# Sending 120 of the last head's 128 output-weight rows to 24 partitions through three DMA engines

## Chip, cores, metric

One core of one Trainium2 chip. The metric is the device time of one execution in microseconds; the median of several executions is quoted, with the lowest and highest. The profile of an execution covers a span some 1.8 us shorter than its time.

## The reference

A decode step for four sequences: attention of 32 query heads over 8 key/value heads and a window of 1024 positions, an output projection `wo`, and beside it a small MLP whose result gates the attention's.

```python
xn = _layernorm(x)                       # x: (4, 1, 512)
s = _A_ref(xn, k_cache, v_cache, wq, wo) # q = xn @ wq; softmax(q k^T) v; ... @ wo, wo: (4096, 512)
g = _silu(_B_ref(xn, w1, b1, w2, b2))    # layernorm, w1, gelu, w2
return x + s * g
```

Some 28.8 MB are read: keys and values 16.8 MB, `wq` and `wo` 4.2 MB each, `w1` and `w2` 1.8 MB each. The tolerance of the comparison is wide against `s * g`. So "correct" says little about a row put in the wrong place.

## The kernel before

All large loads go through SyncE's DMA queue, one after the other: keys, values, MLP weights, and `wo` last. The 4096 rows of `wo` lie as eight groups (one per key/value head) of 128 partitions x 4 rows, in six loads; the last group is cut in two, so that less work follows the last landing.

```python
wo_r = A_wo.rearrange("(g p i) o -> p g i o", g=HKV, i=4)
for n, (g0, g1, i0, i1) in enumerate(((0, 2, 0, 4), (2, 4, 0, 4), (4, 6, 0, 4), (6, 7, 0, 4),
                                      (7, 8, 0, 3), (7, 8, 3, 4))):
    d_wo.append((g0, g1, i0, i1, pg.dma("sp", ...)))      # cut: the load of these groups and rows

def to_rows(g0, g1):         # attention output (128 dims x heads) -> the rows' order, on PE
    ...                      # cut: 16 matmuls with selector weights, then one copy to OW (DVE)

def wo(k, rows):             # a tile's four 128-column pieces are the weights, OW is streamed (4 columns)
    for g in range(g0, g1):
        for i in range(i0, i1):
            for c in range(4):
                pe.matmul(psM[:, PS_W + c * 4:PS_W + (c + 1) * 4],
                          wo_sb[:, g, i, c * 128:(c + 1) * 128], OW[:, i, g * 4:(g + 1) * 4], ...)
```

That is 16 selection matmuls and 128 output matmuls at the end of PE's work; then a product with the gate, a transpose, the sum with `x` and the store.

The softmax here doesn't subtract the row's maximum and nothing guards it: scores larger than these inputs give would overflow.

Of the kernel before, what the change touches and what calls it, by code (L numbers as in the profile page):

```python
# [16 lines left out]
class _Program:  # L17
# [10 lines left out]
    def add(self, eng, fn, *deps):  # L28
        op = _Op(eng, fn, deps)
        self.ops[eng].append(op)  # L30
        return op
# [42 lines left out]
def bass_recurrent_scan__sliding_block_cached__mixer_channel_mlp__decode_kernel(  # L74
# [14 lines left out]
    ALU = mybir.AluOpType  # L89
    AF = mybir.ActivationFunctionType  # L90
    AX = mybir.AxisListType
    BF16 = dt.bfloat16
    F32 = dt.float32

    B, D = 4, 512
    HQ, HKV, DH = 32, 8, 128
# [12 lines left out]
    NB = 3  # L109
# [6 lines left out]
    sb = nc.alloc_sbuf_tensor  # L116
# [5 lines left out]
    wo_sb = sb([128, HKV, 4, D], BF16)  # L122
    w1_sb = sb([128, 4, F], BF16)
    w2_sb = sb([128, FC, D], BF16)
    kt_buf = sb([128, NKT, UT * 128], BF16)
    P_buf = sb([128, HKV, NC * 16], BF16)

# [18 lines left out]
    ones_bf = sb([128, 128], BF16)  # L146
# [12 lines left out]
    b2_sb = sb([4, 128], BF16)  # L159
    sel = sb([128, 4, 32], BF16)  # L160
    OW = sb([128, 4, HKV * 4], BF16)
    hT = sb([128, 64], BF16)

    OTb = sb([128, HKV * 16], BF16)
# [10 lines left out]
    psS = [nc.alloc_psum_tensor("psS%d" % i, [128, 512], F32) for i in range(2)]  # L175
    psO = [nc.alloc_psum_tensor("psO%d" % i, [128, 512], F32) for i in range(2)]
    psM = nc.alloc_psum_tensor("psM", [128, 512], F32)
    PS_Z, PS_W = 192, 208

    pg = _Program(nc)  # L180
    add = pg.add
# [3 lines left out]
    d_b1 = pg.dma("act", "b1", lambda e: e.dma_start(  # L185
        b1_sb[0:1, :], B_b1.rearrange("(o n) -> o n", o=1)))
# [17 lines left out]
    def load_v(g):  # L204
        d_v[g] = pg.dma("sp", "v%d" % g, lambda e: e.dma_start(  # L205
            kv_buf[:, (HKV + g) % NS, :, :].rearrange("p c d -> p (c d)"), cache_rows(A_v_cache, g)),
            t_last[(HKV + g) % NS] if HKV + g >= NS else None)
# [11 lines left out]
    for g in range(2, HKV):  # L219
# [4 lines left out]
    c_1 = add("gp", lambda e: e.memset(ones_bf[:, :], 1.0))  # L224
    c_id = add("gp", lambda e: e.affine_select(
        ident[:, :], ones_bf[:, :], [[1, 128]], ALU.is_equal, 0.0,
        base=0, channel_multiplier=-1), c_1)
    c_ind = add("gp", lambda e: e.affine_select(
        ind[:, :], ones_bf[:, :], [[0, 32], [1, 4]], ALU.is_equal, 0.0,
        base=0, channel_multiplier=-1), c_1)  # L230
    c_sel = add("gp", lambda e: e.affine_select(
        sel[:, :, :], ones_bf[:, :], [[1, 4], [4, 32]], ALU.is_equal, 0.0,
        base=0, channel_multiplier=-1), c_1)
    c_xT = add("gp", lambda e: e.memset(xT[:, :, :], 0.0))
    c_yT = add("gp", lambda e: e.memset(yT[:, :, :], 0.0))
    c_z = add("gp", lambda e: e.memset(zero_bf[:, :], 0.0))
# [2 lines left out]
        base=0, channel_multiplier=-1), c_z)  # L239
    c_o32 = add("gp", lambda e: e.memset(ones32[:, :], 1.0))  # L240
    c_id32 = add("gp", lambda e: e.affine_select(
        ident32[:, :], ones32[:, :], [[1, 128]], ALU.is_equal, 0.0,
        base=0, channel_multiplier=-1), c_o32)


    v = add("dve", lambda e: e.tensor_copy(x32[:, :], x_bf[:, :]), d_x)  # L246
# [3 lines left out]
    a = add("act", lambda e: e.activation(sq1[:, :], vt1[:, :], AF.Sqrt), v)  # L250
# [9 lines left out]
    a = add("act", lambda e: e.activation(sq2[:, :], vt2[:, :], AF.Sqrt), v)  # L260
# [5 lines left out]
    cp = {}  # L266
    sc = {}
    ex = [None] * HKV
    den = [None] * HKV
    ep = [None] * HKV  # L270
# [54 lines left out]
    def epilogue(g):  # L325
        pso = psO[g % 2]
        cs = slice(g * 16, (g + 1) * 16)
        v = add("dve", lambda e: e.tensor_reduce(  # L328
            den_sb[:, cs], bass.AP(psS[g % 2], 0, [[512, 128], [1, 16], [16, NC]]),
            AX.X, ALU.add), den[g])  # L330
        v = add("dve", lambda e: e.reciprocal(rden[:, cs], den_sb[:, cs]), v)  # L331

        ep[g] = add("dve", lambda e: e.tensor_tensor(  # L333
            bass.AP(OTb, g * 16, [[HKV * 16, 128], [1, 4], [4, 4]]),
            pso[:, 0:16], rden[:, cs], ALU.mult), v, pv_op[g])


    v_xyT = None
# [3 lines left out]
    def f_xy(pe):  # L342
# [10 lines left out]
    v_xyT = add("dve", lambda e: e.tensor_copy(  # L353
        yT[:, :, 0:4], psK[1][:, 16:32].rearrange("p (c b) -> p c b", c=4)), t_xy, c_yT)
# [32 lines left out]
    mlp = {}  # L387

    def f32k(n):

        return kt_buf[:, n, :].bitcast(F32)
# [3 lines left out]
    def mlp1():  # L395
        def fn(pe):
            last = None
            for c in range(4):
                for s in range(4):
                    pe.matmul(psK[0][32 * s:32 * s + 32, 0:1024].bitcast(F32), yT[:, c, :],  # L400
                              bass.AP(w1_sb, c * F + K0[s], [[4 * F, 128], [1, 4], [FC, 128]]),
                              start=(c == 0), stop=False, tile_position=(0, 32 * s))
            for s in range(4):
                last = pe.matmul(psK[0][32 * s:32 * s + 32, 0:1024].bitcast(F32),
                                 ones_bf[0:1, 0:32],
                                 bass.AP(b1_sb, K0[s], [[F, 1], [1, 4], [FC, 128]]),
                                 start=False, stop=True, tile_position=(0, 32 * s))
            return last
        t = add("pe", fn, v_xyT, d_w1, d_b1, *[cp[n] for n in range(NUN - NB, NUN)])
        a = add("act", lambda e: e.activation(f32k(0), h_ps, AF.Square), t)  # L410
        v = add("dve", lambda e: e.scalar_tensor_tensor(f32k(1), f32k(0), 1.0 / GELU_K, h_ps,  # L411
                                                        op0=ALU.add, op1=ALU.mult), a)
        mlp["t"] = add("act", lambda e: e.activation(f32k(2), f32k(1), AF.Tanh,
                                                     scale=GELU_C * GELU_K), v)
# [41 lines left out]
    NUN = HKV * NU  # L456
    for n in range(LAG, NUN + LAG):
# [4 lines left out]
    d_w1 = pg.dma("sp", "w1", lambda e: e.dma_start(  # L462
        w1_sb[:, :, :], B_w1.rearrange("(p c) f -> p c f", c=4)))
# [2 lines left out]
        w2_sb[:, :, :], B_w2.rearrange("(p c) o -> p c o", c=FC)))  # L466
    for g in range(2, HKV):
        load_v(g)

    wo_r = A_wo.rearrange("(g p i) o -> p g i o", g=HKV, i=4)  # L470
    d_wo = []
    for n, (g0, g1, i0, i1) in enumerate(((0, 2, 0, 4), (2, 4, 0, 4), (4, 6, 0, 4), (6, 7, 0, 4),
                                          (7, 8, 0, 3), (7, 8, 3, 4))):
        d_wo.append((g0, g1, i0, i1, pg.dma("sp", "wo%d" % n, lambda e, g0=g0, g1=g1, i0=i0, i1=i1:
                                            e.dma_start(wo_sb[:, g0:g1, i0:i1, :],  # L475
                                                        wo_r[:, g0:g1, i0:i1, :]))))

    def to_rows(g0, g1):

        psx = psS[0]  # L480

        def fn(pe):
            last = None
            for i in range(4):
                for j in range(4):
                    last = pe.matmul(psx[32 * j:32 * j + 32, i * 32 + g0 * 4:i * 32 + g1 * 4],
                                     sel[:, i, :],
                                     bass.AP(OTb, g0 * 16 + j * 4,
                                             [[HKV * 16, 128], [16, g1 - g0], [1, 4]]),
                                     start=True, stop=True)  # L490
            return last
        t = add("pe", fn, ep[g1 - 1], c_sel, ex[HKV - 2])
        return add("dve", lambda e: e.tensor_copy(
            OW[:, :, g0 * 4:g1 * 4],
            psx[:, 0:128].rearrange("p (i n) -> p i n", i=4)[:, :, g0 * 4:g1 * 4]), t)

    first = [True]

    def wo(k, rows):
        g0, g1, i0, i1, d = d_wo[k]  # L500

        def fn(pe):
            last = None
            for g in range(g0, g1):
                for i in range(i0, i1):
                    for c in range(4):
                        last = pe.matmul(psM[:, PS_W + c * 4:PS_W + (c + 1) * 4],  # L507
                                         wo_sb[:, g, i, c * 128:(c + 1) * 128],
                                         OW[:, i, g * 4:(g + 1) * 4],
                                         start=first[0], stop=(k == len(d_wo) - 1 and i == i1 - 1),  # L510
                                         skip_group_check=True)
                        first[0] = False
            return last
        return add("pe", fn, d, rows, mlp["g"])

    for g in range(HKV):
        PV(g)
        if g == 0:
            epilogue(0)
            mlp1()  # L520
        if g >= 2:
            epilogue(g - 1)
        if g == 1:
            mlp2()
            mlp3()
        if g == 2:
            mlp4()
    epilogue(HKV - 1)
    rows = to_rows(0, HKV)
    for k in range(len(d_wo)):  # L530
        t_w = wo(k, rows)


    v = add("dve", lambda e: e.tensor_tensor(  # L534
# [3 lines left out]
    t = add("pe", lambda pe: pe.transpose(psS[0][0:16, 0:128], sg_sb[:, :], ident32[:, :]),  # L538
            v, c_id32, ex[HKV - 2])
# [56 lines left out]
```

## Time and profile before

| | before |
|---|---|
| time, median of 3 (lowest to highest) | 77.07 us (77.06 to 77.15) |
| span of the profile | 75.3 us |
| landing of the last `wo` load, first and last of 16 engines | 70.42 and 72.17 us |
| last output matmul starts | 72.32 us |
| PE busy, DMA queue busy | 66%, 92% |

Each of SyncE's large loads raises its semaphore 16 times, the page counts 16 DMA engines, and 16 packets of these loads are in flight (at 68.20 us). So I count one rise of the semaphore, a landing, as one engine; the landings in the table are the times of these rises in the trace. They tell how many engines are late, but not which. Lines of the page, the chain of waits, the tail's table and PE's timeline stand in the prediction, with their reading.

### The profile page before, as it was taken

Reading aid. Unit: us, or ns where it says so; the run is one execution under the profiler, and the core shown is the slowest. Engines: PE = TensorE matmul, PEld = TensorE weight load, DVE = VectorE, ACT = ScalarE, POOL = GpSimd, SP = SyncE. Lnnn points to the kernel's source line nnn. Section 1 sums busy time; section 2 is a strip of 40 time slices with the busy share of each in tenths; the row PEclk is TensorE's granted clock in tenths of the full one; section 3 lists DMA queues with packets and bytes.
Section 4 is the critical chain, followed back from the end, with each engine's and each line's share of the span. In section 5 each row is a group of like instructions: output and inputs, shape, how many; then the busy total and the mean of one; then the engine's idle time right before and its main releaser. Section 6 shows DMA issues by size and latency. Waiting matters only on the chain.

```text
span 75.3 us, 2297 instructions
## 1 busy us (share of the span) xinstructions
PE 50.0 (66%) x1046; PEld 39.8 (53%) x1058; DVE 39.3 (52%) x82; ACT 9.8 (13%) x16; POOL 4.6 (6%) x14
## 2 busy tenths in 40 slices
PE   0000039993859949987997994999069879818770
PEld 0000039992359939976997860104049576518740
DVE  0778107786058967985996424001664679770010
ACT  0611000000090303111130630003300000000000
POOL 6980000000000000000000000000000000000000
PEclk9999999999999999999999999569755555555555
DMA  1899999998999999999999999999999999999600
GB/s 36 244 455 405 420 422 479 435 444 370 427 422 431 422 418 431 427 414 466 401 420 453 406 443 390 427 431 409 427 427 440 418 401 416 418 420 416 252 25 2
DMA packets 4219, 28.99 MB, mean 385 GB/s; under 512 B 493, under 2 KB 625, under 8 KB 1650
## 3 DMA queue, kind: packets, MB, share of 16 engines
q1 hardware_dynamic: 4160, 28.84, 92.2%
q8 instruction: 8, 0.13, 0.6%
q10 hardware_dynamic: 50, 0.01, 0.1%
q14 instruction: 1, 0.01, 0.0%
HBM read 28.85 MB, written 0.00 MB: 383 GB/s over the span
## 4 chain that ended last, share of the span: by engine, by line
DMA 36%; PE 35%; SPq 16%; issue 5%; DVE 4%
DMA wo_sb<-in_A_wo_dram 24%; PE psK L278 22%; SPq L475 15%; DMA kv_buf<-in_A_k_cache_dram 12%; PE psS L297 7%; PE psO L362 3%; DVE kt_buf L284 2%; DVE q_sb L368 1%; PE psK L374 1%; PE psM L507 1%; PE psK L346 1%; PE psS L538 1%; SPq L212 1%; SPq L205 0%; DVE o_bf L540 0%
## 5 line engine op out<-in xcount | busy, mean ns | idle before, releaser
L278 PE MATMUL psK<-ident,kv_buf 128*128 128x128 bf16 x256 | 21.2, 237 | 11.8 <-DMA kv_buf<-in_A_k_cache_dram 10.6
L284 DVE COPY kt_buf<-psK 128x1024 bf16<-128x1024 bf16 x32 | 21.3, 691 | 8.7 <-PE psK L278 8.6
L278 PEld LDWEIGHTS psK<-ident,kv_buf 128*128 128x128 bf16 x256 | 17.1, 108 | 11.1 <-DMA kv_buf<-in_A_k_cache_dram 10.6
L297 PE MATMUL psS<-qT,kt_buf 128*128 128x16 bf16 x256 | 10.4, 169 | 1.7 <-issue 1.1
L297 PEld LDWEIGHTS psS<-qT,kt_buf 128*128 128x128 bf16 x256 | 9.4, 96 | 3.0 <-issue 2.1
L315 PEld LDWEIGHTS psO<-P_buf,kv_buf 128*128 128x128 bf16 x256 | 7.4, 102 | 3.0 <-issue 3.0
L315 PE MATMUL psO<-P_buf,kv_buf 128*128 128x16 bf16 x256 | 8.0, 173 | 1.0 <-DVE OTb L333 0.6
L328 DVE TENSOR_REDUCE den_sb<-psS 128x16 f32<-128x512 f32 x8 | 5.5, 691 | 4.2 <-PE psO L315 4.0
L305 ACT ACTIVATE P_buf<-psS 128x512 bf16<-128x512 f32 x8 | 4.8, 597 | 17.1 <-PE psS L297 17.1
L400 PE MATMUL psK<-w_sb,yT 128*32 128x512 bf16 x16 | 4.9, 1093 | 1.3 <-issue 1.3
L507 PE MATMUL psM<-OW,wo_sb 128*128 128x4 bf16 x128 | 3.9, 166 | 1.1 <-issue 0.6
L507 PEld LDWEIGHTS psM<-OW,wo_sb 128*128 128x128 bf16 x128 | 3.6, 104 | 1.4 <-issue 1.2
L411 DVE SCALAR_TENSOR_TENSOR kt_buf<-kt_buf,psK 128x512 f32<-128x512 f32 x1 | 0.7, 686 | 6.4 <-ACT kt_buf L410 6.4
L534 DVE TENSOR_TENSOR sg_sb<-psM,g_sb 128x16 f32<-128x16 f32 x1 | 0.2, 185 | 4.7 <-PE psM L507 4.7
L400 PEld LDWEIGHTS psK<-w_sb,yT 128*32 128x32 bf16 x16 | 0.5, 114 | 3.8 <-issue 3.8
L369 ACT ACTIVATE q_sb<-psO 128x512 bf16<-128x512 f32 x1 | 0.6, 597 | 13.5 <-PE psO L362 13.5
L424 PE MATMUL psK<-ident,kt_buf 128*128 128x128 bf16 x4 | 0.6, 307 | 2.4 <-DVE kt_buf L419 2.4
L331 DVE RECIPROCAL rden<-den_sb 128x16 f32<-128x16 f32 x8 | 2.0, 253 | 0.3
L362 PE MATMUL psO<-wq_sb,xT 128*32 128x512 bf16 x32 | 1.9, 380 | 0.3 <-DVE xT L351 0.3
L246 DVE CAST P_buf<-x_bf 4x512 f32<-4x512 bf16 x1 | 0.8, 795 | 2.4 <-DMA x_bf<-in_A_x_dram 2.4
L237 POOL TENSOR_SCALAR_AFFINE_SELECT negm<-zero_bf 128x512 bf16<-128x512 bf16 x1 | 1.9, 1852 | 0.1
L321 PE MATMUL psS<-P_buf,ones_bf 128*128 128x512 bf16 x3 | 1.8, 587 | 0.0
(64 smaller groups left out, 27.4 us busy)
## 6 DMA issues: line engine op xcount, KB each, us to landing
kv_buf<-in_A_k_cache_dram SPq DMA_DIRECT2D x8, 1024.0 KB, 19.9
kv_buf<-in_A_v_cache_dram SPq DMA_DIRECT2D x8, 1024.0 KB, 22.8
wq_sb<-in_A_wq_dram SPq DMA_DIRECT2D x2, 2048.0 KB, 11.3
w_sb<-in_B_w_dram SPq DMA_DIRECT2D x2, 1792.0 KB, 27.9
wo_sb<-in_A_wo_dram SPq DMA_DIRECT2D x3, 1024.0 KB, 24.3
wo_sb<-in_A_wo_dram SPq DMA_DIRECT2D x1, 512.0 KB, 21.5
wo_sb<-in_A_wo_dram SPq DMA_DIRECT2D x1, 384.0 KB, 18.2
wo_sb<-in_A_wo_dram SPq DMA_DIRECT2D x1, 128.0 KB, 18.0
```

Source lines behind the costliest of these rows:

```text
L237: c_neg = add("gp", lambda e: e.affine_select(negm[:, :], zero_bf[:, :], [[0, 32], [1, 4], [0, 4]], ALU.is_equal, NEG, base=0, channel_mul ...
L278: last = pe.transpose(psK[n % NB][:, j * 128:(j + 1) * 128], kv_buf[:, g, u * UT + j, :], ident[:, :])
L284: cp[n] = add("dve", lambda e: e.tensor_copy(kt_buf[:, n % NKT, :], psK[n % NB][:, 0:1024]), t, sc.get(n - NKT))
L297: last = pe.matmul(psS[g % 2][:, c * 16:(c + 1) * 16], kt_buf[:, n % NKT, j * 128:(j + 1) * 128], qT[:, g * 16:(g + 1) * 16], start=False, ...
L305: ex[g] = add("act", lambda e: e.activation(P_buf[:, g, :], psS[g % 2][:, 0:512], AF.Exp, scale=SCALE), sc[n])
L315: last = pe.matmul(pso[:, 0:16], kv_buf[:, (HKV + g) % NS, c, :], P_buf[:, g, c * 16:(c + 1) * 16], start=(c == 0), stop=(c == NC - 1))
L328: v = add("dve", lambda e: e.tensor_reduce(den_sb[:, cs], bass.AP(psS[g % 2], 0, [[512, 128], [1, 16], [16, NC]]), AX.X, ALU.add), den[g])
L331: v = add("dve", lambda e: e.reciprocal(rden[:, cs], den_sb[:, cs]), v)
L362: last = pe.matmul(psO[m // 4][32 * s:32 * s + 32, 0:512], xT[:, c, :], wq_sb[:, c, m * 512:(m + 1) * 512], start=(c == 0), stop=(c == 3), ...
L400: pe.matmul(psK[0][32 * s:32 * s + 32, 0:1024].bitcast(F32), yT[:, c, :], bass.AP(w1_sb, c * F + K0[s], [[4 * F, 128], [1, 4], [FC, 128]]) ...
L475: e.dma_start(wo_sb[:, g0:g1, i0:i1, :], wo_r[:, g0:g1, i0:i1, :]))))
L507: last = pe.matmul(psM[:, PS_W + c * 4:PS_W + (c + 1) * 4], wo_sb[:, g, i, c * 128:(c + 1) * 128], OW[:, i, g * 4:(g + 1) * 4], start=firs ...
```

## The change

Half of the DMA engines finish some 1.4 us ahead of the others: the last load's landings before are eight at 70.42 to 70.73 us and eight at 71.37 to 72.17. The change takes the 128 rows of the last head from the load that all 16 engines share, and gives 120 of them to a load on three engines, meant to be ones that finish early. The load has 24 partitions of five rows; its source pattern has an outer size of 3. The other eight rows go by a small load. The group's other three heads then lie as three rows per partition. The buffer is that of the first MLP weights, so these loads wait for the matmuls that read it.

```diff
+    wox_sb = w1_sb[0:24, :, :].rearrange("p c f -> p (c f)")[:, 0:6 * D].rearrange("p (j o) -> p j o", j=6)
...
+    R3 = (7 * 512 + 384) * D
+    d_wox = [pg.dma("sp", "wox0", lambda e: e.dma_start(
+        wox_sb[:, 0:5, :].rearrange("p j o -> p (j o)"),
+        bass.AP(A_wo.tensor, R3, [[5 * D, 3], [15 * D, 8], [1, 5 * D]])), mlp["w1"]),
+        pg.dma("sp", "wox1", lambda e: e.dma_start(
+            wox_sb[0:8, 5, :], bass.AP(A_wo.tensor, R3 + 120 * D, [[D, 8], [1, D]])), mlp["w1"])]
+    load_wo(3, 6, 7, 0, 4)
+    w3_r = A_wo[7 * 512:7 * 512 + 384, :].rearrange("(p i) o -> p i o", i=3)
+    d_w3 = [...]     # cut: rows 0 and 1 of each partition, then row 2
...
+            for i in range(3):        # selection for the group of three rows: 9 matmuls more
+                for j in range(3): ...
+            for a in range(6): ...    # and for the 24 partitions: 6 more
...
+        if n == 2:                    # output matmuls of the 24-partition tile: 24, after the third load's
+            wo([(wox_sb[:, a, :], OWx[:, a * 4:(a + 1) * 4], False, False) for a in range(5)]
+               + [(wox_sb[0:8, 5, :], OWx[0:8, 20:24], False, False)], rows[2], *d_wox)
```

PE has 31 selection matmuls in place of 16, and 148 output matmuls in place of 128.

More of the change, by code (lines that the diff above doesn't have):

```diff
@@ L124, in bass_recurrent_scan__sliding_block_cached__mixer_channel_mlp__decode_kernel @@
     w2_sb = sb([128, FC, D], BF16)
+    wox_sb = w1_sb[0:24, :, :].rearrange("p c f -> p (c f)")[:, 0:6 * D].rearrange(
+        "p (j o) -> p j o", j=6)
     kt_buf = sb([128, NKT, UT * 128], BF16)
@@ L161, in bass_recurrent_scan__sliding_block_cached__mixer_channel_mlp__decode_kernel @@
     OW = sb([128, 4, HKV * 4], BF16)
+    sel3 = sb([128, 3, 3, 128], BF16)
+    selx = sb([128, 6, 24], BF16)
+    OW3 = sb([128, 12], BF16)
+    OWx = sb([24, 24], BF16)
     hT = sb([128, 64], BF16)
@@ L243, in bass_recurrent_scan__sliding_block_cached__mixer_channel_mlp__decode_kernel @@
         base=0, channel_multiplier=-1), c_o32)
+    ones_w = bass.AP(ones_bf, 0, [[128, 128], [0, 9], [1, 128]])
+    c_sel3 = add("gp", lambda e: e.affine_select(
+        sel3[:, :, :, :], ones_w, [[-128, 3], [1, 3], [3, 128]], ALU.is_equal, 0.0,
+        base=0, channel_multiplier=-1), c_1)
+    c_sx = add("gp", lambda e: e.affine_select(
+        selx[:, 0:5, :], ones_bf[:, 0:120], [[1, 5], [5, 3], [15, 8]], ALU.is_equal, 0.0,
+        base=0, channel_multiplier=-1), c_1)
+    c_sx5 = add("gp", lambda e: e.affine_select(
+        selx[:, 5, :], ones_bf[:, 0:24], [[1, 24]], ALU.is_equal, 0.0,
+        base=120, channel_multiplier=-1), c_1)
     v = add("dve", lambda e: e.tensor_copy(x32[:, :], x_bf[:, :]), d_x)
@@ L408, in fn @@
             return last
-        t = add("pe", fn, v_xyT, d_w1, d_b1, *[cp[n] for n in range(NUN - NB, NUN)])
+        t = mlp["w1"] = add("pe", fn, v_xyT, d_w1, d_b1, *[cp[n] for n in range(NUN - NB, NUN)])
         a = add("act", lambda e: e.activation(f32k(0), h_ps, AF.Square), t)
@@ L468, in bass_recurrent_scan__sliding_block_cached__mixer_channel_mlp__decode_kernel @@
         load_v(g)
-    wo_r = A_wo.rearrange("(g p i) o -> p g i o", g=HKV, i=4)
-    d_wo = []
-    for n, (g0, g1, i0, i1) in enumerate(((0, 2, 0, 4), (2, 4, 0, 4), (4, 6, 0, 4), (6, 7, 0, 4),
-                                          (7, 8, 0, 3), (7, 8, 3, 4))):
-        d_wo.append((g0, g1, i0, i1, pg.dma("sp", "wo%d" % n, lambda e, g0=g0, g1=g1, i0=i0, i1=i1:
-                                            e.dma_start(wo_sb[:, g0:g1, i0:i1, :],
-                                                        wo_r[:, g0:g1, i0:i1, :]))))
-    def to_rows(g0, g1):
-        psx = psS[0]
-        def fn(pe):
-            last = None
-            for i in range(4):
-                for j in range(4):
-                    last = pe.matmul(psx[32 * j:32 * j + 32, i * 32 + g0 * 4:i * 32 + g1 * 4],
-                                     sel[:, i, :],
-                                     bass.AP(OTb, g0 * 16 + j * 4,
-                                             [[HKV * 16, 128], [16, g1 - g0], [1, 4]]),
-                                     start=True, stop=True)
-            return last
-        t = add("pe", fn, ep[g1 - 1], c_sel, ex[HKV - 2])
-        return add("dve", lambda e: e.tensor_copy(
-            OW[:, :, g0 * 4:g1 * 4],
-            psx[:, 0:128].rearrange("p (i n) -> p i n", i=4)[:, :, g0 * 4:g1 * 4]), t)
-    first = [True]
-    def wo(k, rows):
-        g0, g1, i0, i1, d = d_wo[k]
-        def fn(pe):
-            last = None
-            for g in range(g0, g1):
-                for i in range(i0, i1):
-                    for c in range(4):
-                        last = pe.matmul(psM[:, PS_W + c * 4:PS_W + (c + 1) * 4],
-                                         wo_sb[:, g, i, c * 128:(c + 1) * 128],
-                                         OW[:, i, g * 4:(g + 1) * 4],
-                                         start=first[0], stop=(k == len(d_wo) - 1 and i == i1 - 1),
-                                         skip_group_check=True)
-                        first[0] = False
-            return last
-        return add("pe", fn, d, rows, mlp["g"])
     for g in range(HKV):
@@ L528, in bass_recurrent_scan__sliding_block_cached__mixer_channel_mlp__decode_kernel, with load_wo @@
     epilogue(HKV - 1)
-    rows = to_rows(0, HKV)
-    for k in range(len(d_wo)):
-        t_w = wo(k, rows)
+    wo_r = A_wo.rearrange("(g p i) o -> p g i o", g=HKV, i=4)
+    d_wo = []
+    def load_wo(n, g0, g1, i0, i1):
+        d_wo.append((g0, g1, i0, i1, pg.dma("sp", "wo%d" % n, lambda e: e.dma_start(
+            wo_sb[:, g0:g1, i0:i1, :], wo_r[:, g0:g1, i0:i1, :]))))
+    for n, g0 in enumerate((0, 2, 4)):
+        load_wo(n, g0, g0 + 2, 0, 4)
+    R3 = (7 * 512 + 384) * D
[4 more added lines that the diff above has]
+            wox_sb[0:8, 5, :], bass.AP(A_wo.tensor, R3 + 120 * D, [[D, 8], [1, D]])), mlp["w1"])]
@@ new lines, in bass_recurrent_scan__sliding_block_cached__mixer_channel_mlp__decode_kernel, with to_rows, fn @@
+    load_wo(3, 6, 7, 0, 4)
+    w3_r = A_wo[7 * 512:7 * 512 + 384, :].rearrange("(p i) o -> p i o", i=3)
+    d_w3 = [(i0, i1, pg.dma("sp", "w3%d" % i0, lambda e, i0=i0, i1=i1: e.dma_start(
+        wo_sb[:, 7, i0:i1, :], w3_r[:, i0:i1, :]))) for i0, i1 in ((0, 2), (2, 3))]
+    def to_rows():
+        psx = psS[0]
+        def fn(pe):
+            last = None
+            for i in range(4):
+                for j in range(4):
+                    last = pe.matmul(psx[32 * j:32 * j + 32, i * 28:(i + 1) * 28],
+                                     sel[:, i, :],
+                                     bass.AP(OTb, j * 4, [[HKV * 16, 128], [16, 7], [1, 4]]),
+                                     start=True, stop=True)
+            o = 7 * 16
+            for i in range(3):
+                for j in range(3):
+                    last = pe.matmul(psx[:, 128 + i * 4:132 + i * 4], sel3[:, j, i, :],
+                                     OTb[:, o + j * 4:o + j * 4 + 4],
+                                     start=(j == 0), stop=(j == 2))
+            for a in range(6):
+                last = pe.matmul(psx[0:24, 160 + a * 4:164 + a * 4], selx[:, a, :],
+                                 OTb[:, o + 12:o + 16], start=True, stop=True)
+            return last
+        t = add("pe", fn, ep[HKV - 1], c_sel, c_sel3, c_sx, c_sx5, ex[HKV - 2])
+        return [add("dve", lambda e: e.tensor_copy(
+            OW[:, :, 0:28], psx[:, 0:112].rearrange("p (i n) -> p i n", i=4)), t),
+            add("dve", lambda e: e.tensor_copy(OW3[:, :], psx[:, 128:140]), t),
+            add("dve", lambda e: e.tensor_copy(OWx[:, :], psx[0:24, 160:184]), t)]
@@ new lines, in wo, with fn @@
+    def wo(tiles, *deps):
+        def fn(pe):
+            last = None
+            for w, o, st, sp in tiles:
+                for c in range(4):
+                    last = pe.matmul(psM[:, PS_W + c * 4:PS_W + (c + 1) * 4],
+                                     w[:, c * 128:(c + 1) * 128], o,
+                                     start=(st and c == 0), stop=sp, skip_group_check=True)
+            return last
+        return add("pe", fn, *deps)
+    rows = to_rows()
+    for n, (g0, g1, i0, i1, d) in enumerate(d_wo):
+        wo([(wo_sb[:, g, i, :], OW[:, i, g * 4:(g + 1) * 4], n == 0 and g == 0 and i == 0, False)
+            for g in range(g0, g1) for i in range(i0, i1)], d, rows[0], mlp["g"])
+        if n == 2:
+            wo([(wox_sb[:, a, :], OWx[:, a * 4:(a + 1) * 4], False, False) for a in range(5)]
+               + [(wox_sb[0:8, 5, :], OWx[0:8, 20:24], False, False)], rows[2], *d_wox)
@@ L534, in bass_recurrent_scan__sliding_block_cached__mixer_channel_mlp__decode_kernel @@
+    for i0, i1, d in d_w3:
+        t_w = wo([(wo_sb[:, 7, i, :], OW3[:, i * 4:(i + 1) * 4], False, i == 2)
+                  for i in range(i0, i1)], d, rows[1])
     v = add("dve", lambda e: e.tensor_tensor(
```

## The prediction

Two passages are cut out of it, because no trace shows what they say: one that says what the packets of the kind "instruction" are for, and one with rules for these packets, for the engines that a load gets and for the spacing of matmuls. That the load would go to three engines was thus my assumption; the trace after shows three landings and 24 packets of 5 KB. No term of the sum is cut: 70.13 + 109 x 0.0267 = 73.04 us against 72.32, and 77.07 + 0.71 = 77.8 us. "Refill" is no more than a name: a packet of the kind "instruction" in the trace, and the stop of PE that ends after it. In the trace before such stops follow the packets that start at 25.51, 32.21, 38.29 and 67.84 us, and end 2.2 to 2.4 us after these starts, at PE's instructions 450, 706, 962 and 1986. That PE waits for the packet is inferred from these times.

> **What bounds the kernel now.** I read the page first, then the chain of waits, then the tail (from 67 us on) in the timeline, in a table by stretches, and in the trace's records of transfers.
>
> The page says that all 16 DMA engines are busy almost to the end, and that in the last slices they thin out.
>
> ```profile
> PE   0000039993859949987997994999069879818770
> DMA  1899999998999999999999999999999999999600
> GB/s 36 244 455 405 420 422 479 435 444 370 427 422 431 422 418 431 427 414 466 401 420 453 406 443 390 427 431 409 427 427 440 418 401 416 418 420 416 252 25 2
> ```
>
> Each slice is 1.88 us. PE is at seven tenths in the last slices before the end: the DMA queue is not alone there. The chain of waits ends like this:
>
> ```profile
> 53.69 18.16 DMA wo_sb<-in_A_wo_dram
> 71.86 0.05 issue
> 71.90 0.60 PE psM L507 x16
> 72.50 0.02 issue
> 72.52 0.20 DVE sg_sb L534
> ```
>
> So the end hangs on the landing at 71.86 us of the fifth output-weight load (three of the four rows per partition of the last group), then on 16 matmuls, then on 2.8 us of epilogue and store that the change leaves alone. The landings behind it come from the 16 counts of each transfer's semaphore in the trace. The sixth load's lie in two groups: eight engines at 70.42 to 70.73 us, eight at 71.37 to 72.17. The table by stretches shows the same, with half of the DMA share left after 70.13 us:
>
> ```profile
> 68.00:69.55 1.55, 1.55 (x53) 1.49 (x54) 0.00 (x0) 0.00 (x0) 0.00 (x0) 0.50 0.98 392
> 69.55:70.13 0.58, 0.00 (x0) 0.00 (x0) 0.00 (x0) 0.00 (x0) 0.00 (x0) 0.50 1.05 415
> 70.13:71.86 1.73, 1.72 (x59) 1.63 (x58) 0.00 (x0) 0.00 (x0) 0.00 (x0) 0.50 0.49 185
> ```
>
> (Columns: stretch, length, busy us of PE, PEld, DVE, ACT and POOL with counts, TensorE clock, DMA share, GB/s.) This is what the change is after: move bytes from the late engines to early ones. But the PE column matters more to me. PE works from 68.00 to 69.55, stands still for 0.58 us, and works on to 71.86: it is almost as late as the data. The timeline of PE:
>
> ```profile
> 67.19 0.30 PE L486 MATMUL psS<-OTb,sel 128*32 128x32 bf16 x16 [1.30 <-DVE OTb L333]
> 68.00 1.55 PE L507 MATMUL psM<-OW,wo_sb 128*128 128x4 bf16 x53 [0.51 <-DVE OW L493]
> 70.13 2.35 PE L507 MATMUL psM<-OW,wo_sb 128*128 128x4 bf16 x75 [0.58 <-issue]
> ```
>
> The 53 matmuls take 1.55 us of which the last one's own 0.166 is latency: (1.55 - 0.166) / 52 = 26.7 ns each. Of the 75, the 59 that need earlier loads start by 70.13 + 58 x 0.0267 = 71.68; then PE waits 0.2 us for the landing. So PE has only 0.2 us of slack.
>
> **The gap of 0.58 us** has no releaser ("issue") and falls in the middle of the second load's matmuls (53 = 32 + 21). I counted the instructions that the trace has on PE (weight load, matmul, semaphore) before such gaps: 450, 706, 962 and 1986, all 256 apart or a multiple of it. The queue table has eight packets of the kind "instruction", of 16 KB each; they start at 25.51, 32.21, 38.29 and, for the last gap, 67.84 us, and these four gaps end at 27.95, 34.43, 40.45 and 70.13, always 2.2 to 2.4 us later.
>
> ```profile
> q8 instruction: 8, 0.13, 0.6%
> ```
>
> [...]
>
> [...]
>
> **The change part by part.**
> 1. DMA bytes. The last group's 512 rows were 8 x (3 KB + 1 KB) per engine; now 384 rows go as 8 x (2 KB + 1 KB), and 120 of the other 128 as eight packets of 5 KB on each of three engines, eight more as 1 KB on each of eight engines. The transfer records give medians of 159 ns for 4 KB, 121 for 3 KB and 46 for 1 KB. From these I estimate 84 for 2 KB and 199 for 5 KB. Per engine: before 8 x (121 + 46) = 1.34 us, after 8 x (84 + 46) = 1.04: all but three engines end 0.25 to 0.3 us sooner. The three get 8 x 0.199 + 0.05 - 0.3 = 1.3 us more. If they are of the early group they end at 70.6 + 1.3 = 71.9, level with the late group's new end at 71.9. Taken alone this is worth 0.25 us.
> 2. Issue. The load of the 24 partitions lands where the first MLP weights lay, so SyncE waits for their last matmul, which the timeline ends at about 51.7 us; before, SyncE issued its fourth output-weight load at 49.4. The landings are 16 us later, so the queue stays full. No cost.
> 3. Row selection on PE: 31 matmuls in place of 16. The 16 took 0.30 us; the nine of 128 columns at 26.7 ns and six small ones add about 0.3 us before the copy to OW. The first output-weight matmul starts at about 68.3 us. Two more copies on DVE, of some 0.2 us, are needed only later.
> 4. Output matmuls on PE: 28 x 4 + 24 + 12 = 148 in place of 128.
> 5. GpSimd builds three more selectors at the start: by 1.85 us for 512 columns, about 4.2 us for the 1152 and 0.6 for the others. It ended at 5.5 us, so ends near 10.5, before DVE's first large copy at 11.7, and is needed at 67. No cost.
>
> **The sum on PE.** Nothing before the row selection changes on PE (the comparison of instruction order shows the same sequence up to there), so the refill boundary stays at instruction 1986, 69 matmuls after the last attention matmul. Before, that was 16 + 53; after, 31 + 38. The 38 are done at 68.3 + 38 x 0.0267 = 69.3, and PE waits for the same refill until about 70.13. So the later start is hidden, but 148 - 38 = 110 matmuls remain where 75 did. Their last start is 70.13 + 109 x 0.0267 = 73.04, against 72.32 before: **+0.7 us**. All data are there by then (71.9), so the DMA gain is not seen. 77.07 + 0.71 = 77.8 us.
>
> **The rivals.**
> - DMA still sets the end. For: the chain ends in a landing. Against: 0.2 us of slack on PE against 35 more matmuls. It would need the refill to come early enough to stall nothing; PE would then end at 68.3 + 147 x 0.0267 + 0.17 = 72.4, and the kernel take 76.8 to 77.0 us.
> - The three engines are not early ones. Each refill delays one engine by about 1.1 us (one more of the 16 landings falls behind after each), and I cannot name the engines. If one of the three is late, its last landing is 72.05 + 1.3 = 73.4 and the end 1.0 to 1.2 us later: 78.1 to 78.3 us. The author chose the three, presumably because they are early, so I give this one in five.
> - A ninth stall. Its boundary would be instruction 2242; the trace has 2139 on PE, the change adds 70 and a few waits: about 2213. It should not come; if it did, the refill that starts at 71.74 would hold PE until 74.0, and the time be near 78.6.
> - SyncE's wait delays the queue: against it stand the 16 us above.
>
> **Range and chances.** The main case is 77.8 us, the DMA-bound one 76.8 to 77.0, the late-engine one up to 78.3. I say **77.75 us**, 77.0 to 78.3 eight times in ten. Two per cent is 1.54 us: none of the likely cases reaches it. Faster 0.01, within 2% 0.95, slower 0.04.
>
> **What would show it.** Right: the chain of waits ends in PE output matmuls without a DMA landing just before; the "issue" gap lies after 38 of them and ends near 70.1; about 110 follow without a break; the last landing comes near 71.9 and before PE's end; the row selection takes about 0.3 us more. Wrong: a landing of the 24-partition load or of the last load after 72.5 us that PE waits for (late engines); no gap, or one that ends before 69.5 (the refill theory is off); a second gap near 73 us.

## The result, and the profile after

| | before | after |
|---|---|---|
| time, median of 4 (lowest to highest) | 77.11 us (77.06 to 77.15) | 77.92 us (77.65 to 78.01) |
| span of the profile | 75.3 us | 75.8 us |
| landing of the third `wo` load, last engine | 69.86 us | 70.32 us |
| landing of the last `wo` load, last engine | 72.17 us | 72.75 us |
| last output matmul starts | 72.32 us | 72.90 us |

The ratio is 1.010 (95% interval 1.0074 to 1.0126): under the two per cent that count as slower here, but clear of the noise. Here and below a ratio is the mean time of one kernel's fast runs over that of the other's fast runs of the same rounds, so not quite the ratio of the medians quoted.

The time is what was forecast. The profile is not. The chain of waits of the changed kernel, its end:

```profile
45.04 25.28 DMA wo_sb<-in_A_wo_dram
70.32 0.05 issue
70.36 2.71 PE psM L559 x84
73.08 0.02 issue
73.10 0.20 DVE sg_sb L577
```

84 matmuls run without a long break up to the end, but what released them is a landing, the third load's, and not a refill. PE's timeline (start, length, engine and line, idle time before in brackets; cut: the other 15 selection matmuls, and DVE):

```profile
65.13 0.30 PE L533 MATMUL psS<-OTb,sel 128*32 128x28 bf16 x16 [1.30 <-DVE OTb L352]
66.45 2.08 PE L559 MATMUL psM<-OW,wo_sb 128*128 128x4 bf16 x64 [0.46 <-DVE OWx L551]
70.36 1.01 PE L559 MATMUL psM<-OW,wo_sb 128*128 128x4 bf16 x32 [1.83 <-DMA wo_sb<-in_A_wo_dram]
71.31 0.80 PE L559 MATMUL psM<-OWx,w_sb 24*128 24x4 bf16 x24
72.04 1.03 PE L559 MATMUL psM<-OW,wo_sb 128*128 128x4 bf16 x28
```

PE came to the row selection two microseconds earlier than in the trace before (65.13 against 67.19 us) and idled 1.83 us for data. The refill that was to hold it until 70.1 us began at 65.26 us rather than 67.84, and cost only 0.2 us, between 67.48 and 67.69 us: after exactly 38 output matmuls, as worked out, with 110 left. And the loads were late: the last landing came 0.6 us later than before, not 0.3 sooner. The last four matmuls waited for it, from 72.71 to 72.80 us.

The loads were late because every packet slowed down for a while. In the table by stretches (columns as in the prediction; the last two are DMA share and GB/s), first the kernel before, then the changed one:

```profile
68.00:69.00 1.00, 1.00 (x38) 1.00 (x39) 0.00 (x0) 0.00 (x0) 0.00 (x0) 0.50 1.01 406
69.00:70.00 1.00, 0.55 (x21) 0.49 (x19) 0.00 (x0) 0.00 (x0) 0.00 (x0) 0.50 0.97 386
```

```profile
68.00:69.00 1.00, 0.54 (x21) 0.45 (x17) 0.00 (x0) 0.00 (x0) 0.00 (x0) 0.50 1.02 398
69.00:70.00 1.00, 0.00 (x0) 0.00 (x0) 0.00 (x0) 0.00 (x0) 0.00 (x0) 0.50 1.09 278
```

From 69 to 70 us the engines are as busy as ever and move 278 GB/s in place of 386. So the DMA share stayed full (1.09 against 0.97) while the bytes fell: the packets took longer, and the engines were not idle. The records of single packets say the same: packets of 4 KB take 159 ns in the median throughout the tail of the kernel before; in the changed one those that start from 69.0 to 69.5 us have a median of 262 ns, those of 2 KB 136 in place of the 84 outside this stretch, those of 1 KB 80 in place of 46. That is 1.6 to 1.7 times as long at every size; over the whole stretch from 69.0 to 70.4 us the medians are 251, 126 and 66 ns, 1.4 to 1.6 times; at 69.2, 69.4 and 69.6 us all 16 packets in flight are slow. I call this stretch the spell. For the runs below I count slow packets: those on SyncE's queue after 10 us that took over 15 ns more than the undisturbed median of their size. The kernel before has 12 (ten of them start within 0.03 us of the end of an instruction packet), the changed one 125.

### The profile page after: what moved, and what is told of

Its sections match the earlier page's. It is cut to its first block, busy times and chain, and to the rows that moved or that the text cites. A ratio compares the mean times of both kernels' runs of the same rounds, so it can differ in the third digit from the quotient of the medians.

```text
span 75.8 us, 2387 instructions
## 1 busy us (share of the span) xinstructions
PE 52.3 (69%) x1093; PEld 40.0 (53%) x1093; DVE 39.1 (52%) x84; ACT 9.8 (13%) x16; POOL 6.5 (9%) x17
## 4 chain that ended last, share of the span: by engine, by line
DMA 46%; PE 35%; SPq 8%; DVE 6%; issue 2%
DMA wo_sb<-in_A_wo_dram 33%; PE psK L297 19%; DMA kv_buf<-in_A_k_cache_dram 12%; SPq L507 7%; PE psS L316 6%; DVE kt_buf L303 5%; PE psM L559 4%; PE psO L381 3%; PE psS L312 2%; DVE q_sb L387 1%; PE psK L393 1%; PE psK L365 1%; PE psS L581 1%; SPq L219 1%; SPq L212 0%
## 5 line engine op out<-in xcount | busy, mean ns | idle before, releaser
L297 PE MATMUL psK<-ident,kv_buf 128*128 128x128 bf16 x256 | 20.3, 229 | 11.4 <-DMA kv_buf<-in_A_k_cache_dram 10.7
L297 PEld LDWEIGHTS psK<-ident,kv_buf 128*128 128x128 bf16 x256 | 16.0, 103 | 11.8 <-DMA kv_buf<-in_A_k_cache_dram 10.7
L340 PE MATMUL psS<-P_buf,ones_bf 128*128 128x512 bf16 x8 | 4.3, 534 | 0.0
L312 PE MATMUL psS<-negm,ind 128*128 128x512 bf16 x8 | 3.0, 380 | 0.0
```

Of the source, the lines that this page charges most:

```text
L297: last = pe.transpose(psK[n % NB][:, j * 128:(j + 1) * 128], kv_buf[:, g, u * UT + j, :], ident[:, :])
L312: pe.matmul(psS[g % 2][:, 0:512], ind[:, :], negm[:, :], start=True, stop=False, skip_group_check=True)
L340: den[g] = add("pe", lambda pe: pe.matmul(psS[g % 2][:, 0:512], ones_bf[:, :], P_buf[:, g, :], start=True, stop=True), ex[HKV - 2 + g % 2] ...
```

## The experiments

Two theories of the 0.8 us. **PE**: the 35 added matmuls stand behind PE's last release, so its work sets the end (the prediction). **DMA**: the three-engine load slows all transfers, so a landing sets the end. The second needs a cause of its own: the place that is read (called the source theory below), the number of engines and the bytes that each carries (load theory), the packet size, or the partitions that are written (destination theory). For the three single runs below (`e2_src`, `e2_hi24`, `e3_before2`) the state is unknown, so their traces are read, and their times show little.

### The changed kernel again, and its parts

`e1_after2`: no edit.

> The changed kernel once more, for a second trace. In its first trace the end is set twice over: 84 output matmuls follow the landing of the third output-weight load at 70.32 us without a long break, and the last landing comes at 72.75 us, 0.6 us later than before, because all packets between 69.0 and 70.4 us took 1.65 times their usual time. PE theory (the prediction): a second trace shows again about 84 to 110 matmuls without a long break up to the end, and a time of 77.7 to 78.0 us whether or not packets are slow. DMA theory: the slow spell comes again with the three-engine load in flight, and the end follows the last landing. If the slow spell is chance, it is gone here.

Measured: 77.60 us (77.41 to 77.93) against 77.06, ratio 1.0086 (1.0061 to 1.0112). The spell is back (the 1.65 times of the expectation is the median of the 4 KB packets that start from 69.0 to 69.5 us): 115 slow packets, third load at 70.05, last landing 72.61 us; PE again runs its last 84 matmuls from that third landing, at 70.10 us. So the spell is no chance. The time is a little under the 77.7 us that the PE theory gave. The two theories are not told apart, since both ends come together.

`e1_k12`: twelve engines for three, PE unchanged.

```diff
-        bass.AP(A_wo.tensor, R3, [[5 * D, 3], [15 * D, 8], [1, 5 * D]])), mlp["w1"]),
+        bass.AP(A_wo.tensor, R3, [[5 * D, 24], [1, 5 * D]])), mlp["w1"]),
```

> Same kernel, PE work unchanged to the instruction; only the source pattern of the 24-partition load has 24 as its outer size[...]. PE theory: the time stays at 77.7 to 78.0 us. DMA theory (three engines carry too much, or slow the others): faster by 0.3 us or more, since the last landing returns to about 72.2 us.

Measured: 77.63 us (77.47 to 77.71), ratio 1.0074 (1.0057 to 1.009), 122 slow packets, last landing 72.66 us. The load's semaphore shows 12 landings, which I count as 12 engines. The time hardly moved, as the PE theory had it, but the spell stayed: this shows only that at these partitions it is not the number of engines that makes it.

`e1_no_x_pe`: the PE work of the 24-partition tile left out (30 matmuls), loads kept. Its output is wrong, which doesn't matter for the time.

```diff
-            for a in range(6):
-                last = pe.matmul(psx[0:24, 160 + a * 4:164 + a * 4], selx[:, a, :], ...)
...
-        if n == 2:
-            wo([(wox_sb[:, a, :], OWx[:, a * 4:(a + 1) * 4], False, False) for a in range(5)] + ...
```

> Wrong result on purpose: all loads as in the changed kernel, but the 24 output matmuls of the 24-partition tile and its 6 selection matmuls and copy are left out. PE theory: 24 x 26.7 ns = 0.6 us comes off the end, 77.2 to 77.3 us, or less where a landing takes over. DMA theory: no change, 77.8 to 78.0 us.

Measured: 77.52 us (77.50 to 77.62), ratio 1.0064 (1.0049 to 1.0079); 112 slow packets, last landing 72.60 us, and PE waits for it with four matmuls left. Nearer to the DMA theory: by the medians, 30 matmuls fewer took off 0.1 us of the 0.5, and the runs of the two kernels overlap (77.41 to 77.93 against 77.50 to 77.62), so even that is not clear of the noise.

`e1_no_x_load`: the two loads left out, PE work kept. Its output is wrong, which doesn't matter for the time.

```diff
-    d_wox = [pg.dma("sp", "wox0", ...), pg.dma("sp", "wox1", ...)]
+    d_wox = []
```

> Wrong result on purpose: the two loads of the 128 rows are left out (128 KB of 28.8 MB less, about 0.3 us of all engines), and PE does all of its matmuls on what the buffer holds. PE theory: the order of PE's work stays, and since the third load still lands at about 69.9 us, 84 matmuls follow: 77.4 to 77.8 us. DMA theory: the slow spell goes and the last landing comes near 71.9 us: 76.8 to 77.0 us.

Measured: 77.52 us, but from 76.85 to 77.98, ratio 1.0055 (0.9992 to 1.0117). The spell is gone (11 slow packets, last landing 71.93 us). The profiled run was one of the longer ones, 77.78 us, and shows what the prediction worked out. PE's timeline of this kernel:

```profile
68.22 1.15 PE L555 MATMUL psM<-OW,wo_sb 128*128 128x4 bf16 x38 [0.46 <-DVE OWx L547]
70.01 1.71 PE L555 MATMUL psM<-OW,wo_sb 128*128 128x4 bf16 x58 [0.64 <-issue]
71.66 0.80 PE L555 MATMUL psM<-OWx,w_sb 24*128 24x4 bf16 x24
72.38 0.91 PE L555 MATMUL psM<-OW,wo_sb 128*128 128x4 bf16 x28
```

38 matmuls, a gap that ends at 70.01 us, 110 without a wait for data, the last start at 73.12 us: worked out were 38, 70.13, 110 and 73.04. Here the refill had begun at 67.70 us, as in the first trace of the kernel before (67.84). So the PE path exists; whether it sets the end depends on when the refills fall (the stop ended at 70.01 us here, at 67.69 and 67.63 in the changed kernel). In the 14 traces PE passes its instruction 1986 anywhere from 67.5 to 70.8 us, while it is always 6.6 to 7.3 us from instruction 1730 to 1986. The other runs of this kernel, down to 76.85 us, left no trace; that earlier refills made them fast is likely, not shown. ("Instruction 1986" is a count of the instructions in the trace, with the few missing matmul records filled in.)

### What makes the spell

These take the kernel without the tile's PE work as their base (77.52 us, 112 slow packets, last landing 72.60 us), so that DMA alone is read. Their outputs are wrong, which doesn't matter for the times.

The runs differ in where the load writes and in its landings. I chose the partitions by an assumption on which engine writes which partitions in a full load. No run shows it and the trace does not number the engines, and in the expectations "the same three engines" is that assumption too: the traces show three landings.

`e2_own12`: the same rows, ten in each of partitions 0 to 11 (the eight-row load moves to other columns of its partitions; cut).

```diff
-        wox_sb[:, 0:5, :].rearrange("p j o -> p (j o)"),
-        bass.AP(A_wo.tensor, R3, [[5 * D, 3], [15 * D, 8], [1, 5 * D]])), mlp["w1"]),
+        w1_sb[0:12, :, :].rearrange("p c f -> p (c f)")[:, 0:10 * D],
+        bass.AP(A_wo.tensor, R3, [[10 * D, 3], [30 * D, 4], [1, 10 * D]])), mlp["w1"]),
```

> Wrong result on purpose, beside the run without the 24-tile's PE work (77.52 us, 112 slow packets, last landing 72.60 us). The same 120 rows from the same three engines, but into 12 partitions of ten rows each[...]. Destination theory[...]: the slow spell goes, under 20 slow packets, last landing near 71.9 us, 76.8 to 77.1 us. Source theory (reading these rows, or any rows with three engines, slows HBM) and load theory (three engines too many bytes): unchanged, over 80 slow packets, 77.4 to 77.6 us.

Measured: 76.74 us (76.64 to 76.99) against 76.98, ratio 0.9963 (0.9945 to 0.9981): faster than the kernel before. 13 slow packets, all 12 packets of 10 KB at 385 ns, last landing 72.07 us. The same stretches as above, in this run:

```profile
68.00:69.00 1.00, 0.88 (x33) 0.91 (x34) 0.05 (x1) 0.00 (x0) 0.00 (x0) 0.50 0.98 395
69.00:70.00 1.00, 0.43 (x17) 0.35 (x13) 0.00 (x0) 0.00 (x0) 0.00 (x0) 0.50 0.99 387
```

387 GB/s, as in the kernel before. The load theory falls: three engines (three landings) carry the same bytes as before. The three landed at 69.53 to 69.90 us. They carry 4 x 0.385 = 1.54 us more than the others, and the third load, just before, had landed on the eight early engines by 68.27 us, on the late ones from 68.99: so the three are of the early group.

`e2_src`: the same destination, other rows.

```diff
-        bass.AP(A_wo.tensor, R3, [[5 * D, 3], [15 * D, 8], [1, 5 * D]])), mlp["w1"]),
+        bass.AP(A_wq.tensor, 0, [[5 * D, 3], [15 * D, 8], [1, 5 * D]])), mlp["w1"]),
```

> Wrong result on purpose: as the run without the 24-tile's PE work, but the 120 rows are read from the query weights, at another place in memory. Source theory: the slow spell goes or changes much. Destination theory: it stays, over 80 slow packets between 68 and 70.5 us, last landing 72.5 to 72.8 us.

Measured, one run: 127 slow packets, 118 of them after 68 us, last landing 72.89 us, 77.80 us. The spell does not depend on the place that is read.

`e2_p120`: one row per partition, 15 engines (15 landings).

```diff
-        wox_sb[:, 0:5, :].rearrange("p j o -> p (j o)"),
-        bass.AP(A_wo.tensor, R3, [[5 * D, 3], [15 * D, 8], [1, 5 * D]])), mlp["w1"]),
+        w1_sb[0:120, :, :].rearrange("p c f -> p (c f)")[:, 0:D],
+        bass.AP(A_wo.tensor, R3, [[D, 120], [1, D]])), mlp["w1"]),
```

> Wrong result on purpose: the same 120 rows, one per partition into 120 partitions, by 15 engines[...]. Destination theory: bytes are even over the partitions, so few slow packets (under 40) and a last landing at 72.1 to 72.3 us, 77.0 to 77.2 us. Source theory: over 80 slow packets, 77.4 us or more.

Measured: 77.38 us (77.17 to 77.45), ratio 1.0045 (1.0024 to 1.0067), 83 slow packets, last landing 72.43 us. A miss in both directions: the spell is weaker (packets 1.3 times as long at its height, not 1.6 to 1.9) but does not go. The expectation counted only bytes per partition. They are spread, 1 KB on each of 120 partitions against 5 KB on each of 24; that this makes the spell weaker is not shown.

`e2_hi24`: the same 24-partition load, at partitions 96 to 119.

```diff
-        wox_sb[:, 0:5, :].rearrange("p j o -> p (j o)"),
+        w1_sb[96:120, :, :].rearrange("p c f -> p (c f)")[:, 0:5 * D],
```

> Wrong result on purpose: as the run without the 24-tile's PE work, but into partitions 96 to 119 in place of 0 to 23. Destination theory: the spell stays, over 80 slow packets, since these 24 partitions too get 5 KB each beside their own stream. If partitions 0 to 23 are special, it goes.

Measured, one run: 175 slow packets (packets of 5 KB against their usual 196 ns), last landing 73.08 us, 77.89 us. The spell begins already at 68.1 us and is the strongest with three engines:

```profile
68.00:69.00 1.00, 0.54 (x21) 0.55 (x21) 0.35 (x2) 0.00 (x0) 0.00 (x0) 0.50 1.09 260
69.00:70.00 1.00, 0.80 (x30) 0.71 (x27) 0.00 (x0) 0.00 (x0) 0.00 (x0) 0.50 1.01 249
```

So partitions 0 to 23 are not special. Why it is stronger here is not shown.

`e3_shift12`: the 12-partition load moved by four partitions, a control for its larger packets.

```diff
-        w1_sb[0:12, :, :].rearrange("p c f -> p (c f)")[:, 0:10 * D],
+        w1_sb[4:16, :, :].rearrange("p c f -> p (c f)")[:, 0:10 * D],
```

> Wrong result on purpose, a control beside the run with 12 partitions (13 slow packets, 76.74 us): the same 12 packets of 10 KB per three engines, but into partitions 4 to 15[...]. Destination theory: the spell is back, over 60 slow packets, 77.2 us or more. If it was the packet size or the number of partitions that mended the run before: under 20 slow packets, 76.7 us.

Measured: 77.88 us (77.83 to 78.23), ratio 1.0125 (1.0094 to 1.0156) against 0.9963 in place. The time is as expected, the form is not: 36 slow packets (six of them of 10 KB) rather than over 60, but two engines landed late, the last at 73.41 us, and one of the three 12-partition landings came at 71.45 us where the other two came at 69.81 and 69.88. Packets of 10 KB took up to 862 ns instead of 385. Why two engines and not all are late is not shown. So this control shows that packet size and number of partitions alone do not give the time of `e2_own12`; it did not bring back the spell on all engines.

### A version without the spell

`e3_own44`: the changed kernel with its PE work, the 120 rows into partitions 0 to 11 and 32 to 43; the selector gives zeros for the partitions between (cut: the selector and the eight-row load).

```diff
+    d_wox = [pg.dma("sp", "wox%d" % h, lambda e, h=h: e.dma_start(
+        wox_sb[32 * h:32 * h + 12, 0:5, :].rearrange("p j o -> p (j o)"),
+        bass.AP(A_wo.tensor, R3 + 60 * h * D, [[20 * D, 3], [5 * D, 4], [1, 5 * D]])), mlp["w1"])
+        for h in range(2)]
```

> A version meant to give the right result, to beat both: the changed kernel with its PE work kept to the instruction (31 selection and 148 output matmuls), but the 120 rows go by two loads of the three engines into partitions 0 to 11 and 32 to 43[...]; the rows between are met by zero weights. Destination theory: fewer than 20 slow packets, last landing near 72.0 us. Refill theory of the PE tail: where PE passes its instruction 1986 early (67.7 us, as in both traces of the changed kernel) the end follows the landing, 76.7 us; where it passes it late (70.0 us or later) 110 matmuls remain and the end comes at about 73.1 us plus the epilogue, 77.7 to 77.9 us. So the runs should lie in two groups, with none between 77.0 and 77.5 if the refills know only two phases.

Measured: 78.09 us (78.01 to 78.47), ratio 1.0155, 165 slow packets. It was not the experiment that I meant. Each of the two loads has 12 landings and not three: rows 20 apart by three and 5 apart by four are one run of 12 x 5 rows, and with 12 landings for 12 partitions I count 12 engines. It was the worst of all in time. Beside the next run, which writes the same partitions with three landings per load, it shows by accident that the partitions alone do not settle it.

`e4_own44_k3`: the same with rows 5 apart by three and 15 apart by four, which are not one run of rows in that order.

```diff
-        bass.AP(A_wo.tensor, R3 + 60 * h * D, [[20 * D, 3], [5 * D, 4], [1, 5 * D]])), mlp["w1"])
+        bass.AP(A_wo.tensor, R3 + 60 * h * D, [[5 * D, 3], [15 * D, 4], [1, 5 * D]])), mlp["w1"])
```

> The version of the run before last as it was meant. That run had 12 landings where 3 were wanted: its source pattern was contiguous, so the load spread over 12 engines, one partition each[...]. Now the source steps 5 rows by 3, then 15 by 4[...]. PE work as in the changed kernel. Destination theory: 3 landings per load, fewer than 25 slow packets, last landing 71.9 to 72.2 us if the three engines are early ones, and 76.7 to 77.0 us where PE passes instruction 1986 by 69.2 us; 77.6 to 77.9 us in runs that pass it at 70 us. If one of the three engines is a late one, as the last run's landing at 71.45 us suggests for its run, a landing of the 12-partition loads comes after 71 us and the last one near 73.2 us, 77.7 us or more, with few slow packets. If the spell comes back (over 80), the destination theory is wrong.

Measured: three landings per load; 9 slow packets; all 24 packets of 5 KB at 196 ns; last landing 72.07 us. Time 77.01 us against 76.93, ratio 0.9998 (0.997 to 1.0027). One of the six runs, 78.11 us, is over 1.5% above the fastest, counts as slow and is left out; with it the ratio would be some 1.002. Its clock (0.825) is no lower than that of the others (0.816 to 0.832), and a late refill was expected to give 77.6 to 77.9 us, so it may be that case and not a slow chip: it left no trace. Against the changed kernel this is the cleanest pair: three landings, 24 packets of 5 KB and the same PE work, but for the partitions and one load cut in two. The chain of waits of this kernel:

```profile
44.87 24.86 DMA wo_sb<-in_A_wo_dram
69.73 0.05 issue
69.78 2.68 PE psM L561 x84
72.46 0.02 issue
72.48 0.20 DVE sg_sb L579
```

With the loads mended the 84 matmuls after the third landing set the end alone: none of them waits for data, and the last starts at 72.28 us, where the kernel before has 72.32. (In this trace PE passed instruction 1986 at 68.76 us, early enough.) So the version undoes the change's loss and gains nothing over the kernel before. It does not beat both.

`e3_before2`: the kernel before once more.

> The kernel before once more, for a second trace: the instruction refills may fall early or late, as in the other traces, but with 75 output matmuls behind instruction 1986 even a late refill (70.1 us) leaves PE done when the last load lands. Every theory expects 77.0 us, fewer than 20 slow packets and a last landing at 72.1 to 72.3 us.

Measured, one run: 77.18 us, 9 slow packets, last landing 72.38 us. This time PE was early (row selection at 65.46 us in place of 67.19) and waited for three loads in turn:

```profile
69.90 1.02 PE L507 MATMUL psM<-OW,wo_sb 128*128 128x4 bf16 x32 [1.06 <-DMA wo_sb<-in_A_wo_dram]
71.15 0.59 PE L507 MATMUL psM<-OW,wo_sb 128*128 128x4 bf16 x16 [0.23 <-DMA wo_sb<-in_A_wo_dram]
72.09 0.61 PE L507 MATMUL psM<-OW,wo_sb 128*128 128x4 bf16 x16 [0.35 <-DMA wo_sb<-in_A_wo_dram]
```

In these two traces the kernel before takes nearly the same time with a late refill and with an early one: a landing sets its end either way.

### Both causes in one table

Ratios to the kernel before, each from its own rounds (the upper row from one chip, the lower two from two others):

| | with the tile's PE work | without it |
|---|---|---|
| spell (partitions 0 to 23) | 1.0086 (`e1_after2`) | 1.0064 (`e1_no_x_pe`) |
| no spell (partitions 0 to 11, in `e4_own44_k3` also 32 to 43) | 0.9998 (`e4_own44_k3`) | 0.9963 (`e2_own12`) |

Down a column, the spell costs 0.9 to 1.0%, some 0.7 us. Along a row, the ratios differ by 0.2 to 0.35%, some 0.2 us, for the tile's 30 matmuls; but the intervals overlap in both rows, and the lower row compares two chips, so this share is not shown. (The lower right entry also has other packet sizes.) Without either, the better balance is worth 0.37%, 0.3 us: the gain that the change was after, in a kernel that leaves the tile's products out.

## Why the prediction was right or wrong

The time was right: 77.75 us forecast, 77.92 measured, inside 77.0 to 78.3. Its reasons were right in part, and that they gave this time is largely luck: in both traces of the changed kernel the refill cost 0.2 us and did not set the end, and a slowing of all transfers, which was not foreseen, cost about as much. Two of the prediction's own signs of being wrong came true: the gap ended before 69.5 us, and PE waited for a last landing after 72.5.

1. **DMA bytes: wrong in sign.** "All but three engines end 0.25 to 0.3 us sooner." The packet times were well estimated (5 KB: 199 ns forecast, 196 measured outside the spell; 2 KB: 84 and 84), and with the destination mended the last landing is at 72.07 us against 72.17. But the prediction took an engine's time for a packet as fixed by its size. It did not ask where the bytes are written, and the last landing came 0.6 us later, not 0.3 sooner.
2. **"All data are there by then (71.9), so the DMA gain is not seen": this step failed.** They were there at 72.75 and 72.61 us in the two traces, and PE waited for them at the end.
3. **The refill boundary: right in place, wrong in time.** PE stopped after 38 matmuls with 110 left, in the two traces of the changed kernel and in all four others with the same PE work. The stop at instruction 1986 is there in all 14 traces, at 0.2 to 1.2 us. But "PE waits for the same refill until about 70.13" took one trace's refill time for a property of the kernel. It was 67.69 and 67.63 us in the two traces of the changed kernel. In the run without the loads it was 70.01, and there the whole sum held to 0.1 us.
4. **"+0.7 us" on PE: right number by luck, other road.** What stands is that PE's added matmuls follow its last long wait. That was for the third load's landing, with 84 behind it. Their own share is some 0.2 us at most by the table above, and not clear of the noise; the spell's is about 0.7.
5. **Issue: right.** SyncE issued the 24-partition load at 49.62 us, straight after the third `wo` load, and the first MLP matmuls were done by then.
6. **Row selection: under-estimated, hidden.** From its first matmul to the first output matmul it takes 66.45 - 65.13 = 1.32 us against 68.00 - 67.19 = 0.81 before, so 0.5 us more where 0.3 was said. PE then waited for data anyway.
7. **GpSimd: over-estimated, harmless.** The selector of 1152 columns took 1.41 us, not 4.2; GpSimd ended at 7.4 us.
8. **The late-engine rival: not seen.** In `e2_own12` and `e4_own44_k3`, where no spell blurs it, the three engines land by 69.90 and 69.88 us, and the last landing stays at 72.07: they are early ones.

Open: which engines the refills go to, and why the first refill starts anywhere from 21.7 to 25.8 us. Also open is how three engines' writes slow the packets of all 16. The runs show that it hangs on the partitions written (with three landings 13 and 9 slow packets for 0 to 11 without and with 32 to 43, 112 to 127 for 0 to 23, 175 for 96 to 119), and for 0 to 11 and 32 to 43 on the landings too (9 with three per load, 165 with twelve). What ties engines and partitions together is not shown, and no run looks inside. The packet records hold three facts that an answer must fit. The first packets of the load are not slow: of the 24 of 5 KB the first twelve took 196 to 199 ns in the changed kernel, the first eight 196 in `e2_hi24`. Then a few are: at 68.6 and 68.8 us two of the 16 packets in flight in the changed kernel, at some twice their usual time (408 ns for 196, 333 for 159), and at 69.2 all 16. And the eight-row load, into partitions 0 to 7, was there in `e2_own12` and `e4_own44_k3` too and made no spell.

## What to carry to other kernels

Balancing DMA engines by bytes is not enough: here 120 KB by three engines into partitions 0 to 11 cost nothing (13 slow packets, last landing 72.07 us against 72.17), and into partitions 0 to 23 made packets on all engines 1.4 to 1.6 times as long for 1.4 us (125 slow packets against 12, last landing 72.75). Count the landings on its semaphore in the trace: the same outer size of 3 gave 12 landings in `e3_own44` and three in `e4_own44_k3`, 78.09 us against 77.01. A full DMA share with falling GB/s (1.09 and 278 against 0.97 and 386) was the mark of this in the profile. Before work is added behind the last landing, count it in instructions as well: the stop at instruction 1986 was harmless with 75 matmuls behind it (it ended at 70.13 us, in 77.07 us), and set the end with 110 (70.01 us, 77.78 in `e1_no_x_load`); and one trace does not tell when it falls (it ended at 67.69 us in the changed kernel's).
